# Buffers of sums with fixed roles, halved preparation of D, w1's scale on VectorE and a new issue order in the last stage of a Strassen kernel for FNet plus MLP

## The chip, the core and the metric

The kernel runs on one core of a Trainium2 chip. The metric is the device time of one execution in microseconds (us); the kernel before took 1273.54 us, the median of three runs (1272.49, 1273.54, 1277.88). The engines of the core work side by side, each in the order of its own instructions, and wait for one another through semaphores: TensorE (PE; its weight loads are listed as PEld) multiplies matrices, VectorE (DVE) and ScalarE (ACT) work on elements, GpSimd (POOL) and SyncE (SP) mainly issue DMA transfers here.

## What is computed

x is 2048 x 576 (S x D), w1 576 x 4608, w2 4608 x 576, all in float32. The two DFT matrices of the sequence are 2048 x 2048, those of the hidden dimension 576 x 576. Layer normalisation has no gains, and the activation is a ReLU:

```python
def _A_ref(x, dft_seq_re, dft_seq_im, dft_hid_re, dft_hid_im):
    a = jnp.einsum("bsd,ed->bse", x, dft_hid_re)
    b = jnp.einsum("bsd,ed->bse", x, dft_hid_im)
    return jnp.einsum("ts,bse->bte", dft_seq_re, a) - jnp.einsum("ts,bse->bte", dft_seq_im, b)

def _B_ref(x, w1, w2):
    h = jnp.einsum("bsd,df->bsf", x, w1)
    h = jnp.maximum(h, jnp.zeros_like(h))
    return jnp.einsum("bsf,fd->bsd", h, w2)

x = A_x
xn = _layernorm(x, axis=-1)
return x + _A_ref(xn, A_dft_seq_re, A_dft_seq_im, A_dft_hid_re, A_dft_hid_im) + _B_ref(xn, B_w1, B_w2)
```

## The kernel before

**Numbers as pairs.** Every float32 operand of a matmul is split into a high and a low float16 part, after a scaling by a power of two. `split` (ScalarE L182 for the high part, VectorE L183 for the low one) does this; a product is then three matmuls: high with high, high with low, low with high. The scale comes from the largest magnitude of the operand, or from a sum of magnitudes that bounds it: `magnitude` (L115) is a VectorE reduce with absolute values, while `sum_w1` (L575 to L592) and `sum_w2` are one ScalarE pass (Abs) that accumulates the sum. `power` (L117 to L131) takes such a number across the 128 partitions with GpSimd (L121) and makes the power of two with three tiny VectorE instructions.

**Seven products in place of eight.** Most matrix products go by a Strassen-Winograd scheme on 2 x 2 blocks: seven block products, of operands that are sums of blocks. VectorE makes those sums, and combines the products that come out of TensorE's banks in PSUM.

**Stages.** The tokens are cut into four groups g of 512 (index g), the 4608 hidden columns into nine blocks b of 512. Up to about 130 us the kernel normalises and transposes x while it does block 0; block 1 lasts to about 215 us; blocks 2 to 8 then take about 87 us each, four steps (b, g) of about 21.5 us. A step does the first MLP product of its own block and group, in two halves, by `pair_products` (matmuls L444), and, interleaved with it, the seven products of the second MLP matmul of the step before by `mlp2` (matmuls L514). After the blocks come the hidden DFT (`dft1`, L1032 and L1042, 822 to 937 us) and the last stage, the sequence DFT (L1150, 937 us to the end).

**First product of a step, and its banks.** `pair_products` names its products P1 to P7. It has four banks: u, one for each half, and v and w, which both halves share. ScalarE copies a finished product out of a bank and so frees it (L470 after P1, L472 after P6, L473 after P5), or VectorE adds it to what is there (L471 after P2, L474 after P7, L475 after P3). Then `value` (L451 on ScalarE, L452 on VectorE), `end_s` (L455 to L458), `end_hi` (L463, ScalarE, 1024 columns) and `end_lo` (L466, VectorE) make the operands of the second MLP product.

**The second product's sums.** Of the seven products of `mlp2`, numbers 0, 2, 3 and 6 start a new sum: ScalarE copies the product, scaled, into a buffer of 576 columns (L523). The others are added to a buffer by VectorE (L525). After products 1, 4, 5 and 6 the buffer's content is complete, and GpSimd issues a DMA (L527) that adds it to an array in DRAM called `spill`. So a step uses four buffers' worth of sums. There are three buffers (L495: `sum0` and two pieces of `dbuf`), and a counter hands them out in turn. In the last block, group 1 adds other memory to the list, and group 2 again (the trace then names them `sums`).

**Preparation of weights.** While a block runs, the next one's weights are loaded and prepared by small pieces of work in a list, `todo`; `work` takes one piece at each of ten places of a step. `prepare_block` (L702) writes the list: the loads, some empty pieces as a wait, for each half of w1 its scale, its splits and its sums (`sums_w1`), then the same for w2. A function marked `long` is put only where a longer piece fits. `issue_after` ties an instruction's place in the order to an earlier one that the dictionary `order` holds, under a name such as "acc" (the last L525) or "free" (the last copy that freed a bank). In the last block the list prepares D, the hidden DFT's four quarters of 1440 columns each (`load_d`, `power_d`, `split_d`, `scales_d`).

**Last stage.** It runs over 16 units of seven products of 24 matmuls (about 2.95 us a product). `operand(m)` makes the operand of product m: the additions for S1 and S2 (L1093, L1094), S3 (L1096), S4 (L1098), then its split. It is called three products ahead. Each product ends in an addition into the output tile `o` (L1156, VectorE). The four blocks of the next unit's matrices are loaded by SP (L1072) into the buffers c0 to c3 when the unit before has finished with them.

Of the kernel before, what the change touches and what calls it, by code (L numbers as in the profile page):

```python
# [9 lines left out]
F16 = mybir.dt.float16  # L10
# [39 lines left out]
def kernel(  # L50
# [366 lines left out]

    def freed(i):

        order["free"] = i.ins  # L420

    def pair_products(b, g, i):
# [42 lines left out]
        def end_lo():  # L465
# [4 lines left out]
            P1: lambda: freed(nc.scalar.activation(c11, u, AF.Copy)),  # L470
            P2: lambda: tt(c11, v, c11, ALU.add),  # L471
            P6: lambda: freed(nc.scalar.activation(s1, u, AF.Copy)),  # L472
            P5: lambda: freed(nc.scalar.activation(c22, w, AF.Copy)),  # L473
            P7: lambda: tt(c22, u, c22, ALU.add),  # L474
            P3: lambda: tt(r21, w, s1, ALU.add),  # L475
        }
# [16 lines left out]
    places, sums = {}, {(r, j): None for r in range(2) for j in range(2)}  # L493
    turns = itertools.count()
    sumbufs = [mlp.tile([P, 2, EH], F32, name="sum0", bufs=1)] + [  # L495
        dbuf[:, k : k + 2 * EH].rearrange("p (c e) -> p c e", e=EH)
        for k in (2 * W1B, 2 * W1B + 2 * EH)
    ]

    def mlp2(b, g, n):  # L500
# [20 lines left out]
        if b and n in (0, 2, 3, 6):  # L521
            o = sums[row, col] = sumbufs[next(turns) % len(sumbufs)]
            freed(nc.scalar.activation(o, ps, AF.Copy, scale=us[b]))  # L523
        else:
            order["acc"] = nc.vector.scalar_tensor_tensor(o, ps, us[b], o, ALU.mult, ALU.add).ins  # L525
        if b and n not in (0, 2, 3):
# [8 lines left out]
    def max_w1(b, f):  # L535

        i, r = divmod(f, 2)
        if f == 0:
            mx["w1", b], sc["w1", b], pw["w1", b] = cell("mw1"), cell("sw1"), cell("pw1")
        if r == 0:  # L540
            mx["f", b] = cell("mf", 2)
            mx["b", i] = small.tile([P, 1], BF16, tag=f"mb{i}", name=f"mb{b}_{i}")
# [25 lines left out]
    def split_w1b(b, i, c):  # L568

        w, r = w1s[b, i], raws["w1", b, i]  # L570
        src = (r[:, :5], r[:, 7:], r[:, :5], r[:, 5:9])[c]
        k = (slice(0, 5), slice(5, 8), slice(8, 13), slice(13, 17))[c]
        split(w[:, 0, k], w[:, 1, k], src, sc["w1", b][:, i : i + 1])

    def sum_w1(b, i):  # L575

        if i == 0:
            mx["w1", b], sc["w1", b], pw["w1", b] = cell("mw1"), cell("sw1"), cell("pw1")
        if b < BB:
            junk = mlp.tile([P, 5, GH], F32, tag="stage", name=f"j1_{b}_{i}")  # L580
            junk = junk.rearrange("p a b -> p (a b)")
        else:
            junk = w1bufs[b % 2 * 2 + i].bitcast(F16)
            w1s[b, i] = junk.rearrange("p (n k f) -> p n k f", n=2, f=P)
        with tc.issue_after(order["free" if b > BB else "s"]):
            nc.scalar.activation(
                junk[:, : 2 * KT * P].rearrange("p (k f) -> p k f", f=P), raws["w1", b, i], AF.Abs,
                scale=2.0**-10, accum_out=mx["w1", b][:, i : i + 1],
            )
        if b < BB:  # L590
            mx["b", i] = small.tile([P, 1], BF16, tag=f"mb{i}", name=f"mb{b}_{i}")
            nc.vector.tensor_copy(mx["b", i], mx["w1", b][:, i : i + 1])  # L592

# [73 lines left out]
    def prepare_w1(b, i):  # L667
        p = power_w1(b, i)
        if b < BB:
            return [  # L670
                lambda: sum_w1(b, i),
                lambda: None,
                lambda: later(p),
            ], [
                lambda: split_w1(b, 2 * i),
                lambda: split_w1(b, 2 * i + 1),
            ]
# [13 lines left out]
    def prepare_w2(b):  # L691
# [93 lines left out]
    tile_by(2, (0, 1, 2, 3), ps)  # L785
    w[2]()
    weave(stats([4, 5, 6, 7]))
# [20 lines left out]
    tile_by(7, (0, 1), qs)  # L808
    w[4]()
    mlp1_out(0, 1, 0, *qs)  # L810
    for f in w[5:]:
        f()
# [30 lines left out]

    rho = []

    def load_d(j):
        load_raw(("d", j), dft[:, :, j * EH : (j + 1) * EH], [P, KT, EH])

    def power_d(j):
        if j == 0:  # L850
            sc["d"], pw["d"], mx["d"] = cell("sd", 4), cell("pd", 4), cell("md", 4)
        m = slice(j, j + 1)
        with tc.issue_after(order["acc"]):
            magnitude(mx["d"][:, m], raws["d", j])
        yield from power(sc["d"][:, m], pw["d"][:, m], mx["d"][:, m])
# [4 lines left out]

    def split_d(j):
        split(dsp[j][:, 0], dsp[j][:, 1], raws["d", j], sc["d"][:, j : j + 1])

# [47 lines left out]
    for n in range(2, len(steps)):  # L911
        b, g = steps[n]
        pb, pg = steps[n - 1]
        if g == 0 and b:
            if b + 1 < NB:
                todo += prepare_block(b + 1)
            else:
                todo += [lambda: (load_d(0), load_d(1)), lambda: None, new_d, lambda: None]
                for j in range(4):
                    d = power_d(j)  # L920
                    todo += [lambda d=d: next(d), lambda d=d, j=j: (later(d), split_d(j))]
                    if j < 2:
# [5 lines left out]
        if b == NB - 1 and g:  # L928

            size = 2 * EH  # L930
            if g == 1:
                w = mlp.tile([P, 2, 7, EH], F16, tag="w2s", name="sums", bufs=4)
                w = [w.rearrange("p n q e -> p (n q e)").bitcast(F32)]
# [3 lines left out]
            sumbufs[:] = [  # L937
                r[:, k : k + size].rearrange("p (c e) -> p c e", e=EH)
                for r in w for k in range(0, r.shape[1] - size + 1, size)
            ]  # L940
# [194 lines left out]
    for n, (p, kh) in enumerate(units):  # L1135
# [4 lines left out]
        for i, (q, rq, first, row, col) in enumerate(PRODUCTS):  # L1140
            m = n * 7 + i
            if m + AHEAD < 7 * len(units):
                operand(m + AHEAD)
            if first:
# [10 lines left out]
            o = outs[p][:, row, col * EH : (col + 1) * EH]  # L1155
            nc.vector.scalar_tensor_tensor(o, ps, us["c"][:, n : n + 1], o, ALU.mult, ALU.add)  # L1156
            if kh and i in (2, 4, 5, 6):
# [58 lines left out]
```

## Time and profile before

| | us |
|---|---|
| median of the runs | 1273.54 |
| the profiled execution | 1275.82 |
| its span in the trace | 1274.0 |
| TensorE busy | 1243.3 |
| VectorE busy | 1003.3 |
| ScalarE busy | 724.0 |
| GpSimd busy | 144.2 |
| busy in the last stage (937 to 1274): TensorE, VectorE, ScalarE | 331.1, 263.2, 126.6 |
| D's preparation (726 to 776): the same three | 45.8, 42.4, 30.2 |

The span is the time from the first to the last instruction of the one execution that was profiled; that execution's own time is 1.8 us above it. Lines that group instructions read: kernel line, engine, operation, output <- input, shape and type, count | busy time in us, mean ns of one | idle time just before them and what ended it. Waits read: engine, line <- the engine and line waited for: total us, times, longest. Windows give for each stretch its length, each engine's busy time with its number of instructions, TensorE's granted clock (1.00 is full), the DMA engines' busy share and GB/s. Matmuls overlap, and their ends are modelled, so gaps between them are drawn a little too short.

The granted clock of TensorE was 0.996 of full speed over the run.

### The profile page before, as it was taken

The numbers are of one execution on the slowest core, as the hardware profiler recorded it, in microseconds if no ns is written. First come the engines' busy times: TensorE is split into PE (matmuls) and PEld (weight loads), VectorE is DVE, ScalarE is ACT, GpSimd is POOL, SyncE is SP. The second block draws the span as 40 slices with busy tenths as digits, with TensorE's granted clock in tenths as the row PEclk, the third lists the DMA queues.
The fourth block names the chain that finished last, engine by engine and source line by source line (L and its number), as shares of the span: only waits on it lengthen the run. The fifth ranks groups of instructions, "written<-read, shape, count | busy, mean of one in ns | idle before, by whom it ended". The sixth has DMA issues, their size and how long they took to land.

```text
span 1274.0 us, 25494 instructions
## 1 busy us (share of the span) xinstructions
PE 1243.3 (98%) x10396; PEld 990.6 (78%) x10396; DVE 1003.3 (79%) x1875; ACT 724.0 (57%) x1222; POOL 144.2 (11%) x188
## 2 busy tenths in 40 slices
PE   8899999999999999999999989999999999999998
PEld 7665666888888888878878878877777777777776
DVE  8899997778877777778777877556788788878875
ACT  5846566767776667667767656544553333333332
POOL 2310021212111112112121211100000000000000
PEclk9999999999999999999999999999999999999999
DMA  6022466666657665657576585630043434434420
GB/s 244 22 87 67 141 124 142 123 132 141 130 116 151 141 147 117 133 138 135 115 148 142 105 183 94 120 95 1 1 170 98 144 116 153 131 116 136 129 86 20
DMA packets 60806, 150.75 MB, mean 118 GB/s; under 512 B 6288, under 2 KB 21136, under 8 KB 60688
## 3 DMA queue, kind: packets, MB, share of 16 engines
q1 hardware_dynamic: 42256, 111.36, 26.5%
q0 software_dynamic: 18432, 37.76, 22.2%
q8 instruction: 81, 1.33, 0.4%
q14 instruction: 37, 0.30, 0.1%
HBM read 101.91 MB, written 47.19 MB: 117 GB/s over the span
## 4 chain that ended last, share of the span: by engine, by line
PE 73%; DVE 9%; issue 7%; ACT 4%; DMA 4%; POOL 1%; SPq 0%; POOLq 0%; ACTq 0%; DVEq 0%
PE p L1150 25%; PE p L514 20%; PE bank L444 17%; PE pd L1032 8%; PE p L310 3%; DMA spill<-dbuf 2%; DMA spill<-sum 1%; DVE acc L525 1%; ACT h L463 1%; DVE w2s L183 1%; POOL spill L527 1%; DMA c<-in_cre_dram 1%; DVE st L200 1%; ACT f L903 1%; ACT dbuf L182 0%
## 5 line engine op out<-in xcount | busy, mean ns | idle before, releaser
L514 PE MATMUL p<-w2s,h 128*128 128x288 f16 x3024 | 409.2, 286 | 2.8 <-ACT xT L268 1.0
L514 PEld LDWEIGHTS <-h 128*128 128x128 f16 x3024 | 295.2, 98 | 78.8 <-issue 4.3
L1150 PE MATMUL p<-R,cs 128*128 128x288 f16 x2688 | 331.3, 287 | 2.0 <-DVE o L1156 2.0
L1150 PEld LDWEIGHTS <-cs 128*128 128x128 f16 x2688 | 263.7, 98 | 69.4 <-issue 2.1
L182 ACT ACTIVATE cs<-c,sc_c 128x1024 f16<-128x1024 f32 x112 | 128.4, 1148 | 195.1 <-PE p L1150 147.3
L444 PEld LDWEIGHTS <-w1buf 128*128 128x128 f16 x1600 | 156.5, 98 | 29.9 <-issue 8.8
L183 DVE SCALAR_TENSOR_TENSOR cs<-c,sc_c,cs 128x1024 f16<-128x1024 f32 x112 | 143.6, 1282 | 41.6 <-ACT cs L182 41.6
L444 PEld LDWEIGHTS <-dbuf 128*128 128x128 f16 x1200 | 117.4, 98 | 19.3 <-issue 3.6
L444 PE MATMUL bank<-xT,w1buf 128*128 128x256 f16 x832 | 109.9, 273 | 1.8 <-DVE s L458 1.8
L444 PE MATMUL bank<-acc,w1buf 128*128 128x256 f16 x768 | 102.1, 272 | 5.2 <-ACT s L472 4.5
L466 DVE TENSOR_TENSOR h<-s,h 128x1024 f16<-128x1024 f32 x56 | 68.5, 1224 | 46.2 <-ACT h L463 46.1
L1032 PE MATMUL pd<-dbuf,xT 128*128 128x288 f16 x832 | 103.8, 286 | 0.0
L1032 PEld LDWEIGHTS <-xT 128*128 128x128 f16 x832 | 80.8, 98 | 22.0 <-issue 1.9
L527 POOL DMA_DIRECT2D spill<-dbuf x74 | 64.1, 867 | 296.9 <-DVE dbuf L525 271.2
L451 ACT ACTIVATE h<-acc 128x256 f16<-128x256 f32 x112 | 46.1, 412 | 82.1 <-DVE acc L474 73.1
L444 PE MATMUL bank<-xT,dbuf 128*128 128x256 f16 x624 | 82.3, 273 | 0.0
L444 PE MATMUL bank<-acc,dbuf 128*128 128x256 f16 x576 | 76.6, 273 | 2.7 <-ACT s L472 2.7
L463 ACT ACTIVATE h<-s 128x1024 f16<-128x1024 f32 x56 | 58.9, 1052 | 30.0 <-DVE s L458 30.0
L1156 DVE SCALAR_TENSOR_TENSOR o<-p,us_c,o 128x288 f32<-128x288 f32 x112 | 57.4, 513 | 19.8 <-PE p L1150 19.0
L523 ACT ACTIVATE dbuf<-p,c_ub 128x576 f32<-128x576 f32 x74 | 53.9, 729 | 23.0 <-PE p L514 17.5
L903 ACT ACTIVATE f<-f 128x1024 f32<-128x1024 f32 x64 | 66.9, 1046 | 0.0
L452 DVE SCALAR_TENSOR_TENSOR h<-acc,h 128x256 f16<-128x256 f32 x112 | 47.4, 423 | 24.4 <-ACT h L451 22.7
(161 smaller groups left out, 1532.9 us busy)
## 6 DMA issues: line engine op xcount, KB each, us to landing
spill<-dbuf POOLq DMA_DIRECT2D x74, 288.0 KB, 5.2
f<-in_cre_dram SPq DMA_DIRECT2D x32, 512.0 KB, 6.0
f<-in_cim_dram SPq DMA_DIRECT2D x32, 512.0 KB, 5.4
c<-in_cre_dram SPq DMA_DIRECT2D x32, 512.0 KB, 4.6
c<-in_cim_dram SPq DMA_DIRECT2D x32, 512.0 KB, 4.8
spill<-sum POOLq DMA_DIRECT2D x38, 288.0 KB, 5.4
raw_w<-in_w_dram SPq DMA_DIRECT2D x17, 640.0 KB, 6.4
raw_w<-in_w_dram SPq DMA_DIRECT2D x18, 576.0 KB, 5.2
```

The source lines that it names most:

```text
L182: nc.scalar.activation(hi, src, AF.Copy, scale=s)
L183: nc.vector.scalar_tensor_tensor(lo, src, s, hi, ALU.mult, ALU.subtract)
L444: nc.tensor.matmul(ps, l, r, start=first and m == 0, stop=m == len(todo) - 1, skip_group_check=not first,)
L463: order["s"] = nc.scalar.activation(hi_s, st[:, 1:], AF.Copy).ins
L466: order["lo"] = nc.vector.tensor_tensor(lo_s, st[:, 1:], hi_s, ALU.subtract).ins
L514: nc.tensor.matmul(ps[:, c], h[:, x, qa, c * P : (c + 1) * P], w[:, y, qb], start=first and i == 0 and j == 0, stop=i == NQ - 1 and j == 2 ...
L523: freed(nc.scalar.activation(o, ps, AF.Copy, scale=us[b]))
L527: nc.gpsimd.dma_start(spill[g, row, col], o, accum_op=ALU.add)
L903: nc.scalar.activation(f, f, AF.Abs, scale=2.0**-10, accum_out=sums_c[:, n, q : q + 1])
L1032: nc.tensor.matmul(ps[j], xT[g][:, kx, c * P : (c + 1) * P], dsp[j][:, hl, k], start=(t % 2 == 0 and n == 0), stop=(t % 2 == 1 and n == le ...
L1150: nc.tensor.matmul(ps, w[:, a, k], r[:, c, rq], start=first and k == 0 and j == 0, stop=k == HK - 1 and j == 2, skip_group_check=not first,)
L1156: nc.vector.scalar_tensor_tensor(o, ps, us["c"][:, n : n + 1], o, ALU.mult, ALU.add)
```

## The change

Four parts.

1. Buffers of sums: the counter goes. A function `sum_buffer(g, n)` gives product n of group g a fixed buffer: with a = g mod 2, products 0 and 6 take buffer a, product 2 takes buffer 2, product 3 takes buffer 1 - a. In the last block only group 1 changes the list, to three pieces of one tile.
2. The scale of w1 from block 1 on: the ScalarE pass `sum_w1` goes; `max_w1`, which block 0 used already, takes its place, with two VectorE reduces of 640 columns and a small one of their two results. From block 2 on they are issued after "vfree", the last VectorE addition that frees a bank or a sum. The pieces of a block's list shift: w1's step becomes two pieces that may stand anywhere, w2's first split and its sums become two pieces, and two empty pieces fewer are waited; the list keeps its length of 39.
3. D in halves: each quarter's magnitude and each split is done in two parts (864 and 576 columns), in pieces of their own, 31 pieces in place of 17.
4. Last stage: for products 1 to 6, the operand three products ahead is issued after the last o addition.

```diff
-    turns = itertools.count()
+    def sum_buffer(g, n):
+        a = g % 2
+        return (a, 2, 1 - a, a)[(0, 2, 3, 6).index(n)]
...
         if b and n in (0, 2, 3, 6):
-            o = sums[row, col] = sumbufs[next(turns) % len(sumbufs)]
+            o = sums[row, col] = sumbufs[sum_buffer(g, n)]
             freed(nc.scalar.activation(o, ps, AF.Copy, scale=us[b]))
         else:
-            order["acc"] = nc.vector.scalar_tensor_tensor(o, ps, us[b], o, ALU.mult, ALU.add).ins
+            add = nc.vector.scalar_tensor_tensor(o, ps, us[b], o, ALU.mult, ALU.add)
+            order["acc"] = order["vfree"] = add.ins
...
-            P2: lambda: tt(c11, v, c11, ALU.add),
+            P2: lambda: freed(tt(c11, v, c11, ALU.add), "vfree"),
...
-            P7: lambda: tt(c22, u, c22, ALU.add),
-            P3: lambda: tt(r21, w, s1, ALU.add),
+            P7: lambda: freed(tt(c22, u, c22, ALU.add), "vfree"),
+            P3: lambda: freed(tt(r21, w, s1, ALU.add), "vfree"),
...
-        magnitude(mx["f", b][:, r : r + 1], raws["w1", b, i][:, r * KT : (r + 1) * KT])
+        with tc.issue_after(order["vfree"]) if b >= BB else nullcontext():
+            magnitude(mx["f", b][:, r : r + 1], raws["w1", b, i][:, r * KT : (r + 1) * KT])
         if r:
-            nc.vector.tensor_reduce(mx["b", i], mx["f", b], AX.X, ALU.max)
+            if b >= BB:
+                m = mx["w1", b][:, i : i + 1]
+            else:
+                m = mx["b", i] = small.tile([P, 1], BF16, tag=f"mb{i}", name=f"mb{b}_{i}")
+            nc.vector.tensor_reduce(m, mx["f", b], AX.X, ALU.max)
...
-    def sum_w1(b, i):
...
-        with tc.issue_after(order["free" if b > BB else "s"]):
-            nc.scalar.activation(
-                junk[:, : 2 * KT * P].rearrange("p (k f) -> p k f", f=P), raws["w1", b, i], AF.Abs,
-                scale=2.0**-10, accum_out=mx["w1", b][:, i : i + 1],
-            )
...
-            long(lambda: (sum_w1(b, i), next(p))),
-            lambda: None,
+            lambda: max_w1(b, 2 * i),
+            lambda: (max_w1(b, 2 * i + 1), next(p)),
...
-        steps += [lambda i=i: (split_w2(b, i, 0), sums_w2(b, i)) for i in range(NQ)]
+        for i in range(NQ):
+            steps += [lambda i=i: split_w2(b, i, 0), lambda i=i: sums_w2(b, i)]
...
-        wait, wait2 = ([lambda: None] * n for n in ((2, 2) if b < BB else (4, 1)))
+        wait, wait2 = ([lambda: None] * n for n in ((2, 2) if b < BB else (3, 0)))
...
+    PARTS_D = (slice(0, 3), slice(3, KT))
...
+    def max_d(j, c):
...
+        with tc.issue_after(order["vfree"]):
+            magnitude(mx["dp"][:, c : c + 1], raws["d", j][:, PARTS_D[c]])
+        if c:
+            nc.vector.tensor_reduce(mx["d"][:, j : j + 1], mx["dp"], AX.X, ALU.max)
...
-    def split_d(j):
-        split(dsp[j][:, 0], dsp[j][:, 1], raws["d", j], sc["d"][:, j : j + 1])
+    def split_d(j, c):
+        k = PARTS_D[c]
+        split(dsp[j][:, 0, k], dsp[j][:, 1, k], raws["d", j][:, k], sc["d"][:, j : j + 1])
...
-                    todo += [lambda d=d: next(d), lambda d=d, j=j: (later(d), split_d(j))]
+                    todo += [lambda j=j: max_d(j, 0), lambda d=d, j=j: (max_d(j, 1), next(d))]
+                    todo += [lambda: None, lambda d=d: later(d)]
+                    todo += [lambda j=j, c=c: split_d(j, c) for c in range(2)]
                     if j < 2:
-                        todo += [lambda j=j: load_d(j + 2), lambda: None]
+                        todo += [lambda j=j: load_d(j + 2)]
...
-            elif g == 2:
-                w = [raw.tile([P, KT, EH], F32, tag="raw", name=f"sums{k}") for k in range(2)]
-                w = [r.rearrange("p k e -> p (k e)") for r in w]
...
             if m + AHEAD < 7 * len(units):
-                operand(m + AHEAD)
+                with tc.issue_after(order["o"]) if 0 < m < 7 else nullcontext():
+                    operand(m + AHEAD)
...
-            nc.vector.scalar_tensor_tensor(o, ps, us["c"][:, n : n + 1], o, ALU.mult, ALU.add)
+            order["o"] = nc.vector.scalar_tensor_tensor(
+                o, ps, us["c"][:, n : n + 1], o, ALU.mult, ALU.add
+            ).ins
```

More of the change, by code (lines that the diff above doesn't have):

```diff
@@ L416, with freed @@
     banks1, ends = [], []
-    def freed(i):
-        order["free"] = i.ins
+    def freed(i, key="free"):
+        order[key] = i.ins
     def pair_products(b, g, i):
@@ L568, in split_w1b @@
     def split_w1b(b, i, c):
+        if c == 0:
+            w = w1bufs[b % 2 * 2 + i].bitcast(F16)
+            w1s[b, i] = w.rearrange("p (n k f) -> p n k f", n=2, f=P)
         w, r = w1s[b, i], raws["w1", b, i]
@@ L809 @@
     w[4]()
+    w[5]()
     mlp1_out(0, 1, 0, *qs)
-    for f in w[5:]:
+    for f in w[6:]:
         f()
@@ L844 @@
     rho = []
+    PARTS_D = (slice(0, 3), slice(3, KT))
     def load_d(j):
         load_raw(("d", j), dft[:, :, j * EH : (j + 1) * EH], [P, KT, EH])
+    def max_d(j, c):
+        if j == c == 0:
+            sc["d"], pw["d"], mx["d"] = cell("sd", 4), cell("pd", 4), cell("md", 4)
+        if c == 0:
+            mx["dp"] = cell("mdp", 2)
+        with tc.issue_after(order["vfree"]):
+            magnitude(mx["dp"][:, c : c + 1], raws["d", j][:, PARTS_D[c]])
+        if c:
+            nc.vector.tensor_reduce(mx["d"][:, j : j + 1], mx["dp"], AX.X, ALU.max)
     def power_d(j):
-        if j == 0:
-            sc["d"], pw["d"], mx["d"] = cell("sd", 4), cell("pd", 4), cell("md", 4)
         m = slice(j, j + 1)
-        with tc.issue_after(order["acc"]):
-            magnitude(mx["d"][:, m], raws["d", j])
         yield from power(sc["d"][:, m], pw["d"][:, m], mx["d"][:, m])
@@ L927 @@
                 weave(stats([(g + 1) * TG + i for i in range(TG)]))
[L928 to L933, printed above, removed]
-            elif g == 2:
-                w = [raw.tile([P, KT, EH], F32, tag="raw", name=f"sums{k}") for k in range(2)]
-                w = [r.rearrange("p k e -> p (k e)") for r in w]
+        if b == NB - 1 and g == 1:
+            w = mlp.tile([P, 2, 7, EH], F16, tag="w2s", name="sums", bufs=4)
+            w = w.rearrange("p n q e -> p (n q e)").bitcast(F32)
             sumbufs[:] = [
-                r[:, k : k + size].rearrange("p (c e) -> p c e", e=EH)
-                for r in w for k in range(0, r.shape[1] - size + 1, size)
+                w[:, k : k + 2 * EH].rearrange("p (c e) -> p c e", e=EH)
+                for k in range(0, 6 * EH, 2 * EH)
             ]
```

16 lines of the change are left out of this document (2 added, 14 removed).

## The prediction, made before the changed kernel ran

> **What bounds the kernel now.** I read the page's first lines, then the waits of TensorE, then the chain of waits through one of those waits, then groups and windows. First the page:
>
> ```profile
> span 1274.0 us, 25494 instructions
> PE 1243.3 (98%) x10396; PEld 990.6 (78%) x10396; DVE 1003.3 (79%) x1875; ACT 724.0 (57%) x1222; POOL 144.2 (11%) x188
> ```
>
> TensorE is busy 98%. Its matmuls are not made fewer here, so an edit can pay only in TensorE's idle time (span less busy: 30.7 us) or cost by adding to it. The waits that make up most of that idle time (us in total, times, longest us):
>
> ```profile
> PE bank L444 <- ACT s L472: 7.1, 6, 1.6
> ...
> PE p L1150 <- DVE o L1156: 2.0, 1, 2.0
> PE bank L444 <- DVE s L458: 1.8, 1, 1.8
> ...
> PE p L514 <- DVE acc L525: 0.8, 2, 0.4
> PE bank L444 <- DVE acc L474: 0.7, 2, 0.5
> ```
>
> The first row in six narrow windows is one wait of 0.4 to 1.6 us at the start of each of blocks 2, 4, 5, 6, 7 and 8 (block 3 has none). In the chain of waits at block 6 (start, us, what), the cause shows:
>
> ```profile
> 551.39 0.87 POOL spill L527
> ...
> 553.57 7.19 DMA spill<-dbuf
> ...
> 560.84 0.07 ACT dbuf L523
> ...
> 561.47 1.05 ACT h L463
> 562.52 0.28 ACT s L472
> ...
> 562.84 0.81 PE bank L444 x6
> ```
>
> Product 0's sum is copied by ScalarE (L523) into a buffer that product 5 of the step before is still spilling; the spill lands at 560.75, though product 0's matmuls ended at 557.69. Behind the copy on ScalarE stands `end_hi` (L463), then the copy that frees product P6's bank (L472), and TensorE waits for it. Last, the operations that change engine or size, and VectorE early on (windows: length, PE, PEld, DVE busy, ...):
>
> ```profile
> L586 ACT ACTIVATE w1buf<-raw_w 128x1280 f16<-128x1280 f32 x8 | 10.1, 1261 | 0.0
> ...
> L115 DVE TENSOR_REDUCE c_md<-raw_d 128x1 f32<-128x1440 f32 x4 | 6.6, 1646 | 0.2 <-DMA raw_d<-in_dft_dram 0.2
> ...
> L115 DVE TENSOR_REDUCE c_mf<-raw_w 128x1 f32<-128x640 f32 x4 | 3.2, 799 | 1.4 <-DMA raw_w<-in_w_dram 1.4
> ...
> 100.00:140.00 40.00, 39.43 (x252) 23.31 (x250) 39.53 (x80) 19.64 (x34) 0.38 (x1) 1.00 0.30 100
> 140.00:180.00 40.00, 40.00 (x251) 23.71 (x250) 39.11 (x78) 25.43 (x43) 4.98 (x6) 1.00 0.54 129
> ...
> 220.00:307.00 87.00, 87.00 (x758) 73.87 (x756) 67.68 (x150) 61.50 (x121) 15.78 (x20) 1.00 0.65 130
> ```
>
> VectorE is full from 60 to 180 us, and has 19 us free in each later block of 87.
>
> **Part 1, fixed roles of the sum buffers.** Four uses a step over three buffers, in turn, give product 0 the buffer that product 2's sum had before it, spilled after product 5. With fixed roles it gets the one spilled after product 4. At block 6 that spill was issued at 551.39 and landed at 555.56, before product 0's matmuls end (557.69): the copy no longer waits. What the six waits are worth: 256-column matmuls start 0.109 us apart but are drawn 0.273 long, so each drawn gap is 0.273 - 0.109 = 0.16 too short: 7.1 + 6 x 0.16 = 8.1. What is late next: product 2's copy now waits for product 5's spill (560.75; the copy ran at 565.2, about 563.7 once the stall is gone: 2.9 us to spare; at block 2, 217.55 against 221.0: 2.2), product 3's copy for product 6's (563.63 against 569.3). Spills and GpSimd's issues keep number and order. I allow 0.5 for steps where a w2 split now stands before L472. Taken: -7.6; ends -8.1 and -0.5 (all but one wait re-appearing at product 2).
>
> **Part 2, w1's scale on VectorE.** It removes 16 ScalarE passes (1.26 + 0.19 us for reading the sum) and two casts (0.14); it adds per piece two reduces of 640 (0.80) and one of two elements (0.13): 1.73 us.
>
> - From block 3 on, two pieces a block: +3.5 us VectorE into 19.3 free, -2.9 ScalarE. Each reduce stands behind an addition that frees a bank, so what is queued behind it is the next addition. The tightest is product 4's L525, before product 6's matmuls, with about 1.25 us of slack against 0.8. Slots are about 2.1 us apart; the first reduce comes four slots (8.6 us) after the loads are queued on SP, one earlier than the ScalarE pass; such loads landed after 6.4 and 8.5 us (552.57 to 559.01, 556.22 to 564.75). Taken 0; ends 0 and 28 reduces x 0.80 = 22.4 (the last rival).
> - Blocks 1 and 2 are prepared where VectorE is full: 4 pieces x 1.73 less two casts = 6.6 us more, against 0.5 + 0.9 free in the windows shown, 3.3 free from 60 to 100 and 6.9 from 180 to 220. What is pushed back is mostly the statistics for x's sums, which nothing needs at once, and ScalarE falls by 5.8 there. Taken 0; ends -2 (`prepare` earlier through a freer ScalarE) and +6.6.
> - Separate slots for a w2 split and its sums take three sums away from ahead of product 4's addition in a block's last step. There TensorE shows five gaps of 0.13 (at block 7, six matmuls end 637.96, the next start 638.09), each 0.29 with the 0.16. Taken -1.0; ends 0 and -1.4.
>
> [...]
>
> **Part 3, D in halves.** Two sizes of one reduce give (1646 - 799) / 800 = 1.06 ns a column, so 864 columns cost 1.04 us and 576 0.73; a split that took 1.72 on VectorE becomes about 1.1 and 0.8. VectorE gains some 0.5 us a quarter in all. Removed: the 1.64 and 1.72 us instructions that stood before bank-freeing additions at 755 to 762 (the 1.8 wait) and 775 (0.5). With the overlap these five gaps are 1.84 + 0.48 + 0.19 + 0.18 + 0.16 = 2.85. The work now takes 31 slots in place of 17, so over three steps, with VectorE free for 50 - 42.4 = 7.6 of the 50 us from 726 on. The SP loads stay in number; the second pair comes a little later. Taken -2.5; ends -2.85 and +0.5.
>
> **Part 4, last stage.** Product 5 waited 2.0 us for the addition L1156 of product 2, which stood behind L1093's addition, itself waiting 3.58 us for a load (landed 951.88). Putting operands 4 to 9 behind the o additions takes that away. But S3 and S4 of unit 0 are made later, so their four buffers come free later, and unit 2's loads, in order on SP, land at about 955.5 to 957.1 in place of 953.15 to 955.67. In the new order of VectorE unit 2's L1097 addition still stands ahead of product 5's and 6's o additions and unit 1's S2. From that landing to product 7's o addition there are four additions of 1.15, two splits of 1.19 and three o additions of 0.43 (start to start at 951.9 to 961): 8.3, so 963.8 to 965.4. Product 9, which needs it, is due four products of 2.95 after 953.61, less the 2.0: 963.4. New wait 0.4 to 2.0. Taken net -0.8; ends -2.0 and +2.0 (loads 2.8 later than I put them).
>
> **The sum**: -7.6 + 0 + 0 - 1.0 - 2.5 - 0.8 = -11.9 on the span of 1274.0, so 1262.1. The profiled run took 1275.82, 1.8 above its span, and the median is 1273.54, 2.3 below that run: 1261.6 against the median, rounded to 1262. All good ends together: 1273.5 - 14.4 = 1259, and with the early stage's -2, 1257. All of parts 3 and 4 lost leaves 1265.5; with the 0.5 for part 1 and part 2's sums lost too, 1267. So its own range is 1257 to 1267.
>
> **The rivals.**
>
> - *The buffer's wait moves.* Product 2's copy waits for product 5's spill if that lands 3 us later than here. For: that spill already takes 7.19 us where w1's loads run beside it, against 4.2 for product 4's. Against: it is 2.2 to 2.9 us to spare at the six places, and ScalarE has slack before product 2's bank is needed. About 1 us each is lost again, 6 in all: 1268.
> - *VectorE bounds the early stage.* All of the 6.6 us falls on TensorE between 60 and 215. For: 39.5 of 40 us busy. Against: TensorE itself is at 39.4 and 40.0 there, so VectorE works ahead of it, and about 11 us are free until 220. 1262 + 6.6 = 1268.6.
> - *The reduces stand before the bank-freeing additions* (slower). VectorE is in order; a reduce that waits for its load, or just runs, holds the next L471, L474 or L525, and TensorE waits its full 0.80: 28 in blocks 2 to 8, 22.4 us, 1284. It ends slower than before from 15 of the 28 on (11.9 / 0.8). For: the waits for L474 and L525 above, the first of which stood behind D's long reduce. Against: from block 2 on 19 us a block are free and each is put just behind such an addition.
> - *The halves change nothing*: TensorE's waits at 748 to 776 only move. For: the copies of L470 keep only about 0.2 us of slack behind a split. 1262 + 2.5 = 1264.5, within the forecast's range.
>
> **Chances.** Forecast with the last rival inside it 0.70; moved buffer wait 0.10; early stage 0.09; slower 0.08; better than 1257, 0.03. 0.5% of the median, about what these measurements tell from no change, is 6.4 us, so faster ends at 1267.2: faster 0.72 (a little of the forecast lies above, the better case below), same 0.19, slower 0.09. The range takes in both 1268 cases and reaches to the middle of a half-paid last rival: 1257 to 1272.
>
> **What would show it.** Part 1: no row "bank L444 <- ACT s L472" at block starts, L523 idle only for TensorE; wrong if L523 waits on a spill at product 2. Part 2: TensorE's busy time at 100 to 220 and the number of matmuls in those windows as before; L471, L474 and L525 releasing TensorE no more often; wrong if they do after an L115 on raw_w. Part 3: no gap over 0.3 from 745 to 780. Part 4: product 5 without a wait and one under 2 us at product 9. The prediction fails if TensorE's idle sum is not near 19 us.

## The result, and the profile after

The changed kernel took 1266.69 us (median of six runs, 1264.25 to 1269.43) against 1273.62 for the kernel before in the same series: the ratio is 0.9941, with a 95% interval of 0.9921 to 0.9961. That is 6.9 us less (5.0 to 10.1 by the interval), inside the range of 1257 to 1272, but 4.7 above the 1262 forecast. The span of the profiled execution fell from 1274.0 to 1266.4. The changed kernel's six runs differ with the granted clock: the three from 1264.25 to 1265.86 have a mean of 0.997 or 0.998, the three from 1267.53 to 1269.43 one of 0.993 to 0.995, and the profiled one (1268.20, 0.993) is among the latter.

The first lines of the page of the changed kernel:

```profile
span 1266.4 us, 25532 instructions
PE 1243.7 (98%) x10396; PEld 991.9 (78%) x10396; DVE 1024.9 (81%) x1933; ACT 707.9 (56%) x1194; POOL 149.2 (12%) x188
```

TensorE is as busy as before (1243.7 against 1243.3); the gain of this pair is idle time, which fell from 30.7 to 22.7 us, where the prediction wanted a sum near 19. VectorE has 21.6 us more, ScalarE 16.1 less, as the move of w1's scale wants. TensorE's waits in the changed kernel, the three rows past 60 us that add up to more than a microsecond and stand at other instructions than before:

```profile
PE p L1155 <- DVE o L1161: 2.1, 1, 2.1
PE p L521 <- DVE h L466: 1.5, 2, 0.8
PE bank L444 <- ACT acc L470: 1.4, 1, 1.4
```

Of the rows that the prediction showed, those of L472, L458, L474 and of product 5's L1156 are gone, and L525's (0.8 us, two times) is down to one of 0.5 at 136 us (L532 now); but the last stage has a wait of the same size again (L1155 and L1161 are the old L1150 and L1156), and two are new. To place the gain I took, for each matmul in the trace, its start to the next start less the usual spacing of its shape, and summed this over stretches. In us, with the kernel before at its own times:

| stretch | before | after | what changed |
|---|---|---|---|
| 0 to 75 | 17.4 | 17.1 | little |
| 75 to 200 | 3.6 | 6.6 | **+3.0**, waits for VectorE (L532) and ScalarE's L268, and TensorE at half its clock from 98.25 to 101.66 |
| 200 to 230, block 2's start | 1.5 | 1.5 | L472's 1.3 gone, L470's 1.6 new |
| 230 to 740, blocks 2 to 7 | 8.4 | 1.7 | -8.2 for five L472 waits and five small gaps, two waits for L466 new |
| 740 to 800, D | 3.6 | -0.1 | -3.7, nothing left |
| 800 to 935 | -2.0 | -2.1 | |
| 935 to the end | 2.4 | 2.6 | one wait went, one came |
| sum | 35.0 | 27.4 | -7.6, as the span |

(A stretch is negative where the matmuls run a little closer than usual.) In the changed kernel's row for 75 to 200 a part is clock and not waiting, as two windows show (length, PE, PEld, DVE, ACT, POOL busy, granted clock, DMA share, GB/s):

```profile
94.83:98.25 3.42, 1.49 (x16) 1.04 (x15) 3.42 (x7) 3.18 (x5) 0.00 (x0) 1.00 0.32 110
98.25:101.66 3.41, 3.41 (x9) 1.00 (x9) 2.62 (x9) 1.31 (x3) 0.00 (x0) 0.50 0.19 68
```

The buffers show in what the copies with which ScalarE starts a sum (products 0, 2, 3 and 6) waited for from 200 to 824 us. Before (L523; us, times):

```profile
  PE p L514: 32.7, 35
  DMA spill<-dbuf: 5.4, 4
  PE bank L444: 4.0, 1
  DMA spill<-sum: 1.4, 1
```

and after (L530), the whole list:

```profile
  PE p L521: 38.9, 49
```

No copy waits for a spill any more, not at product 0 and not at products 2 and 3.

### The profile page after: what moved, and what is told of

Same layout as the page of the kernel before. It is cut to its first block, busy times and chain, and to the rows that moved or that the text cites. A ratio compares the mean times of both kernels' runs of the same rounds, so it can differ in the third digit from the quotient of the medians.

```text
span 1266.4 us, 25532 instructions
## 1 busy us (share of the span) xinstructions
PE 1243.7 (98%) x10396; PEld 991.9 (78%) x10396; DVE 1024.9 (81%) x1933; ACT 707.9 (56%) x1194; POOL 149.2 (12%) x188
## 4 chain that ended last, share of the span: by engine, by line
PE 80%; DVE 11%; DMA 3%; ACT 3%; issue 2%; SPq 1%; ACTq 0%; DVEq 0%
PE p L1155 24%; PE p L521 24%; PE bank L444 23%; PE pd L1036 8%; DMA raw_w<-in_w_dram 1%; PE p L310 1%; DMA c<-in_cre_dram 1%; DVE w2s L183 1%; DVE acc L532 1%; DVE h L354 1%; DVE acc L414 1%; DMA acc<-in_x_dram 1%; DVE h L361 1%; DVE w1buf L183 0%; ACT w2s L182 0%
## 5 line engine op out<-in xcount | busy, mean ns | idle before, releaser
L1155 PE MATMUL p<-R,cs 128*128 128x288 f16 x2688 | 331.3, 287 | 2.1 <-DVE o L1161 2.1
L1155 PEld LDWEIGHTS <-cs 128*128 128x128 f16 x2688 | 263.7, 98 | 69.5 <-issue 2.3
L444 PEld LDWEIGHTS <-w1buf 128*128 128x128 f16 x1600 | 156.5, 98 | 23.0 <-issue 1.6
L444 PEld LDWEIGHTS <-dbuf 128*128 128x128 f16 x1200 | 117.4, 98 | 16.1
L444 PE MATMUL bank<-xT,w1buf 128*128 128x256 f16 x832 | 109.9, 273 | 0.0
L444 PE MATMUL bank<-acc,w1buf 128*128 128x256 f16 x768 | 102.1, 273 | 1.4 <-ACT acc L470 1.4
L466 DVE TENSOR_TENSOR h<-s,h 128x1024 f16<-128x1024 f32 x56 | 68.5, 1224 | 33.9 <-ACT h L463 33.7
L535 POOL DMA_DIRECT2D spill<-dbuf x70 | 61.1, 877 | 233.2 <-DVE dbuf L532 184.3
L444 PE MATMUL bank<-xT,dbuf 128*128 128x256 f16 x624 | 82.5, 273 | 0.0
L444 PE MATMUL bank<-acc,dbuf 128*128 128x256 f16 x576 | 76.6, 273 | 0.0
L1161 DVE SCALAR_TENSOR_TENSOR o<-p,us_c,o 128x288 f32<-128x288 f32 x112 | 57.6, 514 | 20.0 <-PE p L1155 19.8
L530 ACT ACTIVATE dbuf<-p,c_ub 128x576 f32<-128x576 f32 x70 | 51.1, 731 | 15.2 <-PE p L521 14.9
```

Of the source, the lines that this page charges most:

```text
L444: nc.tensor.matmul(ps, l, r, start=first and m == 0, stop=m == len(todo) - 1, skip_group_check=not first,)
L466: order["lo"] = nc.vector.tensor_tensor(lo_s, st[:, 1:], hi_s, ALU.subtract).ins
L535: nc.gpsimd.dma_start(spill[g, row, col], o, accum_op=ALU.add)
L1155: nc.tensor.matmul(ps, w[:, a, k], r[:, c, rq], start=first and k == 0 and j == 0, stop=k == HK - 1 and j == 2, skip_group_check=not first,)
L1161: order["o"] = nc.vector.scalar_tensor_tensor(o, ps, us["c"][:, n : n + 1], o, ALU.mult, ALU.add).ins
```

## Experiments

Each kernel was run beside the kernel before on the same chip, whose median moved between chips (1271.56 for e1 to e4, 1273.48 for e5 to e8, 1272.83 for e9 to e11), so I compare ratios, spans and the stretches above. The changed kernel's ratio, 0.9941, has an interval of 0.0020 to either side, some 2.5 us, and its profiled execution took 1.5 us more than its median: a difference of 4 us from its span alone is not yet a difference of the kernels.

**Part 1 alone (e1).** The kernel before with fixed roles.

```diff
-            o = sums[row, col] = sumbufs[next(turns) % len(sumbufs)]
+            o = sums[row, col] = sumbufs[sum_buffer(g, n)]
```

> The kernel before with part 1 alone (fixed roles of the buffers of sums, and the one tile of the last block). Theory: the six waits of TensorE for L472 (7.1 us as listed, 8.1 with the overlap of the matmuls) are all there was to it, so they go, nothing takes their place at products 2 and 3, and the time falls by 8 us, to about 1265.5. The one at block 2's start goes as well (1.3 us), since VectorE is not more loaded than before. Rival: in the changed kernel part 1 had help from the freer ScalarE (no Abs passes); alone it leaves L530's counterpart L523 waiting for spills at product 2 or 3, or L472 late behind other ScalarE work, and less than 5 us are gained.

Measured: 1265.54 against 1271.56, ratio 0.9953 (0.9937 to 0.9970). In the trace all six L472 waits are gone, block 2's too (its stretch falls from 1.5 to 0.3), and none has come at products 2 and 3. The five gaps of 0.29 and D's waits stay (its list has the L458 row with 1.8 and the L474 row with 0.7, as before). So part 1 stands on its own, and is the greater part of the change's gain. The 6.0 us by the medians are below the 8.1 of the waits, though the interval (3.8 to 8.0) all but reaches it; the span of its profiled run, 1263.7, is 10.3 below. 1.8 of that lies in the last stage, which e1 doesn't change: there its wait was not followed by a stretch at half clock (the granted clock is 1.00 in every window from 940 to 968 us; see the last section).

**w1's scale of blocks 1 and 2 back on ScalarE (e2).**

```diff
         if b < BB:
             return [
-                lambda: max_w1(b, 2 * i),
-                lambda: max_w1(b, 2 * i + 1),
+                lambda: sum_w1(b, i),
...
-            lambda: max_w1(b, 2 * i),
-            lambda: (max_w1(b, 2 * i + 1), next(p)),
+            long(lambda: (sum_w1(b, i), next(p))),    # block 2 alone
```

> The changed kernel with w1's scale of blocks 1 and 2 on ScalarE again (the four passes that fall before 215 us); from block 3 on the reduces stay. Theory: VectorE was full between 75 and 215 us, and the 6.6 us of reduces put there were passed on to TensorE: its excess over its own pace rose from 4.0 to 6.8 us between 75 and 200, and a wait of 1.4 for L470 (ScalarE's copy behind L360, that behind VectorE's backlog) came at block 2's start. All of it goes: 4 us faster than the changed kernel, about 1262.5, the wait for L470 gone. Rival: the early differences come from the shifted list and the scheduler's other order, not from VectorE's load; then they stay, and the time is within 1 us of 1266.7.

Measured: 1264.02, ratio 0.9941 (0.9926 to 0.9956), span 1262.4, 4.0 below the changed kernel's span; but the ratio is the changed kernel's own, so the times of the runs don't show these 4 us. The stretch from 75 to 200 falls from 6.6 to 4.0, block 2's start from 1.5 to 0.2. How VectorE's work reached TensorE is seen in the chain of waits of the changed kernel at block 2's start (start, us, what):

```profile
213.16 0.73 DVE w2s L183
213.90 0.66 DVE acc L414
214.56 0.60 DVE h L354
215.16 0.33 DVE s L356
215.49 0.34 DVE s L357
...
215.85 0.43 DVE s L358
...
216.31 0.03 ACT h L360
...
217.27 0.38 ACT acc L470
...
217.69 1.69 PE bank L444 x14
```

VectorE works without a pause; L358 makes the last operand of block 1's last step, ScalarE's L360 waits for it, and L470, which frees the first bank of block 2, stands behind L360. In e2's chain no VectorE instruction stands there; from 204.92 on it is TensorE itself, and then:

```profile
212.36 0.38 ACT h L360
...
213.20 0.38 ACT acc L470
...
213.62 1.69 PE bank L444 x14
```

VectorE's busy time in the window from 180 to 220 us, first the changed kernel, then e2 (PE, PEld, DVE, ...):

```profile
180.00:220.00 40.00, 38.58 (x258) 24.68 (x257) 37.52 (x74) 28.57 (x50) 6.44 (x8) 1.00 0.64 138
```

```profile
180.00:220.00 40.00, 39.92 (x277) 26.53 (x276) 33.81 (x66) 26.93 (x48) 7.29 (x9) 1.00 0.67 140
```

37.52 of 40 against 33.81: the room that I counted on at 180 to 220 had been filled by work pushed back from before.

How much it costs, other traces tell. Up to 200 us e4, e5 and e6 (below) run the changed kernel's matmuls in the same order. Measured by the same sum from 0 to 200 us against the kernel before, the changed kernel is 2.6 us behind, e6 3.5, e5 1.3 and e4 0.7. The first two have the half clock at about 98 us, the other two haven't. Without the reduces of blocks 1 and 2 the difference is -0.6 to 0.6 (e2, e7, e8, e9, e10). The wait for L470 at block 2's start, 1.2 to 1.4, is in every trace with block 2's reduces and in none without. The pairs on one chip agree: e8 is 2.4 us faster than e5 and differs from it by e2's edit alone, and e2 is 2.7 faster than e4, whose last stage is 0.3 longer. So the reduces cost about 2.4 us, of which 1.3 is that wait. The rest of the 4.0 is mostly the stretch at half clock at 98 us. In the changed kernel it follows 1.93 us of idle TensorE from 94.83 to 98.25, where the kernel before has 1.16 from 94.13 to 97.55; that the gaps which the reduces add bring it on is my estimate from these two numbers. It comes in two of these four traces only: the mean granted clock of the profiled execution is 0.993 in the changed kernel and 0.994 in e6, 0.997 in e4 and 0.996 in e5.

**Block 1 alone back on ScalarE (e11).** As e2, but with the second part of its edit left out; a single execution.

> The changed kernel with w1's scale of block 1 alone on ScalarE again; block 2's reduces stay. Theory: each block's reduces are paid where they run: the gaps between 75 and 135 us (2.8 us over the kernel before) come from block 1's, and the wait of 1.4 for L470 at block 2's start from block 2's. So the first go, the second stays. Rival: the backlog is one, and with half of the reduces gone the wait for L470 goes too, or both are halved.

Measured: span 1262.9. The stretch from 75 to 200 is at 4.2, block 2's start keeps its wait for L470 (1.2). So that wait comes from block 2's reduces: 1.2 to 1.4 us. For block 1's nothing is shown: of the 2.4 us less in the stretch from 75 to 200, most is the half clock that e11 hasn't (its mean granted clock is 0.997 against 0.993), and up to 200 us e11 is 1.1 behind the kernel before, between e4 (0.7) and e5 (1.3), which have block 1's reduces.

**A w2 split and its sums in one piece again (e3).**

```diff
-        for i in range(NQ):
-            steps += [lambda i=i: split_w2(b, i, 0), lambda i=i: sums_w2(b, i)]
+        steps += [lambda i=i: (split_w2(b, i, 0), sums_w2(b, i)) for i in range(NQ)]
...
-        wait, wait2 = ([lambda: None] * n for n in ((2, 2) if b < BB else (3, 0)))
+        wait, wait2 = ([lambda: None] * n for n in ((2, 2) if b < BB else (4, 1)))
```

> The changed kernel with a w2 split and its sums in one piece of the list again (and the two empty pieces back, so that the list keeps its length). Theory: the two new waits of TensorE for L466 in the last steps of blocks 4 and 7 (0.92 us each with the overlap) come from the sums that are now interleaved with L455 to L458 and product 4's addition ahead of L466; they go (-1.8), and the five gaps of 0.29 before product 6 of the kernel before come back (+1.4): net -0.4, about 1266. Rival: they come from the w1 reduces having moved VectorE's later work; then they stay, and the time is 1266.7 to 1268.

Measured: 1266.25, ratio 0.9958 (0.9943 to 0.9973). As expected, both L466 waits are gone and five gaps of 0.29 are back, at 381, 466, 551, 636 and 722 us; they weigh the same, since the stretch from 230 to 740 is at 1.7 with either. But that did not say why only blocks 4 and 7 had the L466 wait. VectorE's timeline of the changed kernel there (start, us, instruction):

```profile
450.61 0.45 DVE L642 TENSOR_TENSOR raw_w<-raw_w 128x288 f32<-128x288 f32 x1
...
453.42 1.11 DVE L183 SCALAR_TENSOR_TENSOR w2s<-raw_w,c_sw,w2s 128x864 f16<-128x864 f32 x1
...
455.87 0.45 DVE L643 TENSOR_TENSOR raw_w<-raw_w 128x288 f32<-128x288 f32 x1
...
456.94 1.22 DVE L466 TENSOR_TENSOR h<-s,h 128x1024 f16<-128x1024 f32 x1
```

Two splits and two sets of sums (L642 to L645) stand here ahead of L466, some two places of the list earlier in the step than in block 3. The list shows the reason: when a place can't take a `long` piece, `work` notes it in `owed`, and a later place takes two pieces. With the new list this count stands at 2, 3 and 0 at the ends of three blocks running, and it is carried from one block to the next. e9 tests this.

**The last stage: products 1 to 13 behind the o additions (e4), and all of them (e5).**

```diff
-                with tc.issue_after(order["o"]) if 0 < m < 7 else nullcontext():
+                with tc.issue_after(order["o"]) if 0 < m < 14 else nullcontext():   # e4
+                with tc.issue_after(order["o"]) if m else nullcontext():            # e5
```

> The changed kernel with the operands issued behind the o additions for products 1 to 13 in place of 1 to 6. Theory: the wait of 2.1 us before product 9 of the last stage comes from unit 2's S2 addition (L1097), which the scheduler put ahead of product 5's o addition and which waits for a load on VectorE; with it behind product 12's, the wait goes and nothing comes for it: 2.1 us faster, about 1264.6. Rival: the late loads themselves bound unit 2, so the wait moves to product 12 to 16: within 0.7 us of the changed kernel.

e4 measured 1266.68, ratio 0.9962 (0.9947 to 0.9977): the wait before product 9 is gone, but one of 2.4 us stands at 976.8. It stands before product 16, and the time is the changed kernel's: place and size are the rival's. The cause is another, since the chain there goes through unit 3's S2 addition, which the scheduler now puts early, before the o addition of a product of unit 1, and which waits for unit 3's load, not unit 2's. My theory of the first wait held, and "nothing comes for it" did not.

> The changed kernel with every operand of the last stage behind the o addition before it (no bound of 7 products). Theory: what waits is always the S2 addition of a coming unit, put tens of us too early by the scheduler; behind product 12 and later nobody is late, since unit 2's blocks landed about 28 us before product 16 is due. So the wait of 2.1 goes, and with it the 14 matmuls at half the granted clock behind it (1.6 us): 3.7 us faster, about 1263, and the granted clock stays at 1.00 through 940 to 1000. Rival: with the sums made later, each unit's S2 operand (two additions, two splits) is late, and small waits before the S2 product of each unit eat 2 us or more.

e5 measured 1262.99, ratio 0.9916 (0.9902 to 0.9931), span 1261.1, and the wait is gone for good. The chain of the changed kernel at that place shows what was taken away:

```profile
942.58 6.61 DMA c<-in_cre_dram
...
949.28 0.10 DVE c L1097
...
950.42 0.51 DVE o L1161
950.93 1.14 DVE c L1097
...
952.10 1.22 DVE c L1098
953.32 0.43 DVE o L1161
953.75 1.13 DVE c L1102
954.88 2.39 DVE cs L183 x2
957.27 0.44 DVE o L1161
957.72 0.04 issue
957.76 4.28 PE p L1155 x20
```

Four additions, two splits and three o additions from the landing at 949.19 to product 9 at 957.76. The load itself was for product 16, 20 us away.

More than the wait was gained (5.3 us by span, 3.2 by the ratios; 1.6 of the span's lies in the stretch before 200 us, where the matmuls are the same and e5 has no half clock at 98 us). In the last stage itself it is 3.9, from 2.6 to -1.3. Windows of the changed kernel after the wait (PE, PEld, DVE, ACT, POOL, then the granted clock):

```profile
958.00:960.00 2.00, 2.00 (x12) 1.28 (x10) 1.26 (x2) 1.05 (x1) 0.00 (x0) 0.60 0.13 14
960.00:962.00 2.00, 2.00 (x11) 1.27 (x10) 1.87 (x2) 1.14 (x2) 0.00 (x0) 0.55 0.86 256
962.00:964.00 2.00, 2.00 (x19) 1.60 (x17) 1.29 (x3) 1.15 (x1) 0.00 (x0) 1.00 0.88 223
```

After the wait TensorE got half its clock for 3.41 us (0.50 in a window from 958.40 to 961.82): 12 and 11 matmuls in 2 us where it does 18 or 19, which costs another 1.6 us. In e5 the clock stays at 1.00 there:

```profile
958.00:960.00 2.00, 2.00 (x19) 1.59 (x17) 1.13 (x2) 2.00 (x2) 0.00 (x0) 1.00 0.85 318
```

**D whole again (e6).** The magnitudes and splits of 1440 columns in 17 pieces, as in the kernel before; the rest as in the changed one.

> The changed kernel with D's magnitudes and splits whole again (17 pieces). Theory: the five gaps of TensorE at 745 to 780 of the kernel before come back (1.84 + 0.48 + three small ones): 2.85 us slower, about 1269.5. Rival: with the buffers' stalls gone and w1's scale moved, VectorE has room there, and less than 1 us comes back.

Measured: 1269.81, ratio 0.9960 (0.9946 to 0.9974), 2.4 us above the changed kernel by the ratios (3.1 by the medians, from two chips), and the intervals overlap; in the trace the stretch of D goes from -0.1 to 2.8. The waits are of the same sum, but at other instructions than before: a row "PE bank L444 <- DVE c_pdi L867" with 1.2 and one "PE bank L444 <- DVE s L475" with 0.9.

**w1's scale on ScalarE everywhere (e7), and e2 with e5 (e8).** e7 is e2's edit for all blocks from 1 on; e8 has the edits of e2 and e5 together.

> The changed kernel with w1's scale on ScalarE for every block from 1 on, the rest of the change kept. Theory: from block 3 on it doesn't matter where the 3.5 us a block are done, since both engines have over 19 us a block free; so this equals e2 within 1 us, about 4 us faster than the changed kernel. Rival: the Abs passes of 1.26 us on ScalarE delay L472 or L463 again, and it is 2 us or more slower than e2.

e7 measured 1264.62, ratio 0.9931 (0.9913 to 0.9949), near e2. But the parts differ: blocks 2 to 7 have no gap at all, not the two of L466 either, and D has 3.0 us of new ones at 759 to 783. Both are what the count would do: in e7's list it stands at 2, 3, 4, 5, 6, 7 and is paid back all at once in D's list.

> The changed kernel with the two edits of e2 and e5 together. Theory: the two costs are apart in time and add up: 4.0 + 3.7 = 7.7 us faster than the changed kernel, about 1259. Rival: the earlier last stage meets loads that are no earlier, and a part of e5's gain is lost: 1261 or more.

e8 measured 1260.59, ratio 0.9894 (0.9880 to 0.9909). The span, 1259.2, is 7.2 below the changed kernel's, against 7.7 expected; by the ratios it is 6.0. The two gains add up, each a little smaller by the ratios than by the spans.

**The count cleared at each block's start (e9, and e10 with the scale on ScalarE).**

```diff
         if g == 0 and b:
+            owed.clear()
             if b + 1 < NB:
```

> The kernel of e8, with the count of pieces owed (places that a long piece skipped) set to nothing at each block's start. Theory: the waits for L466 in the last steps of blocks 4 and 7 alone come from that count: it grows 2, 3, 0 over three blocks, and where it is paid back w2's splits and sums run some two places early and stand together ahead of L466. With the count cleared, every block has the list at the same places, as blocks 3, 5 and 6, which have no gap: the two waits (0.92 each) go, 1.8 us faster than e8, about 1258.8. Rival: the reduces of w1 on VectorE make them, or D's list, which now starts one place later, takes the gain back: no faster than e8.

> The kernel of e9 with w1's scale on ScalarE for all blocks from 1 on. Theory: e7's new gaps of 3 us at 759 to 783 came from the count as well (it grew to 7 by D's list and let pieces of D run two at a place), not from the engine that computes the scale; with the count cleared they go, and this equals e9 within 1 us: from block 3 on the move to VectorE was worth nothing either way. Rival: ScalarE's Abs passes cost by themselves, and this is 2 us or more slower than e9.

e9, on top of e8, measured 1258.18, ratio 0.9882 (0.9865 to 0.9898); e10 1258.28, ratio 0.9886 (0.9871 to 0.9901). Against e8 the times don't separate (the intervals overlap), but the traces do: in both, the stretches from 200 to 800 are at 0.2, -0.4 and -0.1: no L466, no D gaps. For e9 the profile names no wait of TensorE at all between 215 us and the end. So the count made the waits for L466 and e7's gaps, and from block 3 on it is all the same which engine finds w1's scale. e9 beats both kernels: 14.7 us below the one before. Its page:

```profile
span 1256.8 us, 25519 instructions
PE 1237.3 (98%) x10396; PEld 988.9 (79%) x10396; DVE 1015.4 (81%) x1923; ACT 708.6 (56%) x1202; POOL 145.9 (12%) x188
```

## Why the prediction was right, and where it was off

The direction and the range were right, the size was 4.7 us too good, and that the time lies in the range is in part luck: in the sum below, three terms that were too good by 6.0 together meet two that were too cautious by 1.6. One premise was too narrow, too: that an edit can pay only in TensorE's idle time. In the kernel before TensorE is drawn busy all through 954 to 956 us, with 12 matmuls where 19 fit at full clock (958 to 960), so time lost to the clock counts as busy and can be gained. By the prediction's own steps, in the profiled pair:

- **Part 1** was taken at -7.6, and the waits it named (8.1) all went; the moved wait at products 2 and 3, a rival, did not come (L530's list, e1). The overlap of 0.16 per gap belongs in the sum: the six listed waits add up to 7.1, but by the spacing of the matmuls 8.1, and in e1 the two stretches from 200 to 740 fall by 8.0.
- **Part 2, blocks 1 and 2: the step that failed.** It took 0 for 6.6 us of new VectorE work, "what is pushed back is mostly the statistics for x's sums, which nothing needs at once". It cost about 2.4 us in the pairs on one chip and 4.0 in the profiled pair, where a stretch at half clock came with it. So it lies between the 0 taken and the 6.6 of the second rival, whose mechanism it is, at a smaller size. What I used against it, that TensorE was itself at 39.4 and 40.0 of 40, shows that VectorE's lag was just hidden, not that it had slack; and of the "about 11 us free" the greater part lies after 180, where the pushed-back work has to be done before block 2 starts. It is a chain of dependent work with an end, and what was added for block 2 came out at 217 as the wait for L470.
- **Part 2, later blocks.** "Taken 0" for the reduces is shown by e9 against e10 (1258.18 and 1258.28); the last rival, with 28 reduces in front of additions, did not come. The -1.0 for the five gaps was right for them (all five gone, 1.4), but two waits for L466 came in (1.85). By these waits the net is +0.4, by the stretch from 230 to 740 it is 0 (1.7 in e1 and in the changed kernel). The step spoke of the order of work in one block and missed that the list's places differ from block to block by the count carried over.
- **Part 3**, taken at -2.5: all of it came (2.8 comes back in e6's trace; the stretch of D fell by 3.7). The prices fit. Reduces in the changed kernel:

```profile
L115 DVE TENSOR_REDUCE c_mf<-raw_w 128x1 f32<-128x640 f32 x36 | 29.1, 809 | 0.1
...
L115 DVE TENSOR_REDUCE c_mdp<-raw_d 128x1 f32<-128x864 f32 x4 | 4.2, 1046 | 0.0
L115 DVE TENSOR_REDUCE c_mdp<-raw_d 128x1 f32<-128x576 f32 x4 | 3.0, 743 | 0.0
```

  1.04 and 0.73 us had been worked out from two other sizes, 1.05 and 0.74 were measured.
- **Part 4**, taken at -0.8 net, was worth nothing (+0.2). The mechanism and the place of the new wait were as worked out, product 9 behind 8.3 us of VectorE work after a late load; its size was 2.07, just over the upper end of the 0.4 to 2.0, since the load landed at 949.19, which is 956.9 on the clock of the kernel before (7.7 us had been gained by then), the late end of the 955.5 to 957.1. What was missing is that both waits brought 1.6 us at half clock with them, the old one at 954.29 to 957.71 and the new one at 958.40 to 961.82. Each of them cost 3.7, and with both gone (e5) the last stage gains 3.9.

In sum, by the stretches of the profiled pair: 4.0 from the early stage (+3.0 from 75 to 200, +1.3 at block 2's start against e1, -0.3 before 75), 1.0 from part 2's later blocks and 1.0 from part 4 are missing from the gain; 0.4 from part 1 and 1.2 from part 3 are above it. -11.9 becomes -7.5, against -7.6 of the span. The medians fell by 6.9.

## What to carry to other kernels

A ring of buffers should be laid out by which release is oldest when the next use comes: a fixed role for each use took away six waits without a byte more. An engine that is full for a stretch can pass added work on to whoever comes at the end of that stretch, as VectorE did here at block 2's start (busy for 37.52 of the 40 us from 180 to 220, with TensorE's wait of 1.4 for L470 in them), even if the engine it feeds looks busy all the time; free time after the deadline is not cover. And where a scheduler may put instructions early, a waiting one holds what stands behind it on its engine (in the changed kernel L1097 waited 2.79 us for its load, and product 9 then 2.07 us): tying one stretch of them moved the wait to the next unit, and tying all of them removed it. Last, two spans can differ by a stretch at half clock, 1.6 us here, that either kernel may meet: a price taken from one pair of profiles should be checked on other traces with the same code.

## What the runs showed of the hardware

In the traces of the kernel before and of the changed one the granted clock of TensorE is recorded as 1.00 or 0.50, and while the matmuls run it stays at 0.50 for 3.41 us, once for 6.83 (16.33 to 23.15 in the changed kernel). The matmuls of the last stage start 0.12 us apart at 1.00 and 0.24 at 0.50. Within each of the two traces these stretches begin whole multiples of 3.413 us apart: in the kernel before at 19.04, 39.52 and 954.29 us, which is 6 and then 268 such steps, in the changed kernel at 16.33, 40.22, 98.25 and 958.40, which is 7, 17 and 252 of them.

In windows of that length, laid from those starts, TensorE's idle time can be set beside what came next. Between 36 and 1260 us these are the windows of the two traces with the most of it:

| trace | window, us | idle in it, us | granted clock in the next |
|---|---|---|---|
| before | 36.11 to 39.52 | 2.60 | 0.50 |
| changed | 36.81 to 40.22 | 2.30 | 0.50 |
| changed | 954.99 to 958.40 | 2.07 | 0.50 |
| before | 950.88 to 954.29 | 1.96 | 0.50 |
| changed | 94.83 to 98.25 | 1.93 | 0.50 |
| before | 756.32 to 759.73 | 1.64 | 1.00 |

The 1.93 us of the changed kernel are three gaps, of which the longest is 1.06. The last stage's wait in seven traces, with the granted clock recorded behind it:

| run | gap, us | granted clock behind it |
|---|---|---|
| e4 | 2.39 | 0.50 from 978 to 980 |
| e7 | 2.35 | 1.00 from 955 to 964 |
| changed | 2.07 | 0.50 from 958.40 to 961.82 |
| before | 1.96 | 0.50 from 954.29 to 957.71 |
| e3 | 1.94 | 1.00 to 963 |
| e6 | 1.89 | 1.00 to 963 |
| e1 | 1.87 | 1.00 to 968 |

e7's gap is longer than the changed kernel's, and the clock stays at 1.00:

```profile
956.00:958.00 2.00, 2.00 (x18) 1.60 (x17) 1.27 (x2) 2.00 (x3) 0.00 (x0) 1.00 0.67 190
958.00:960.00 2.00, 2.00 (x19) 1.58 (x18) 2.00 (x4) 0.78 (x1) 0.00 (x0) 1.00 0.81 256
```

So the length of a gap alone does not tell whether half a clock follows; what spared e7 was not shown. The changed kernel's wait of 2.07 us cost 3.7 with the half clock behind it, e7's of 2.35 had none behind it. Of the four traces with the same matmuls up to 200 us (the changed kernel, e4, e5, e6) two have such a stretch at about 98 us and two haven't, so a difference of this size between two profiles need not be one of the kernels.
